# Softcap attention with a soft mixture of experts: filler products merged, and half tiles moved four products ahead

## The chip, the cores and the metric

The kernel runs on one core of one Trainium2 chip. The metric is the device time in microseconds of one execution, as the median of several runs. The profile is of one more execution.

A few names: TensorE (PE in the profile) multiplies; a product is a pair of instructions, a weight load (PEld) and the product itself. ScalarE is ACT, VectorE is DVE, GpSimd is POOL, and SyncE (SP) issues most of the loads and all stores. PSUM is the memory that products are written to, in eight banks.

## What is computed

```python
scores = scale * np.matmul(q, k.transpose(0, 1, 3, 2))     # batch 8, 12 heads, seq 448, head_dim 64
scores = cap * np.tanh(scores / cap)
attn = softmax(scores)
x = (attn @ v) reshaped to (3584, 768)

logits = x @ phi                                            # 32 slots = 8 experts x 4
slot_input = softmax(logits over tokens).T @ x
for e in range(8):
    slot_out[e] = np.maximum(slot_input[e] @ w1[e], 0) @ w2[e]    # 768 -> 1024 -> 768
return softmax(logits over slots) @ slot_out                # (3584, 768) float32
```

The output is 3584 x 768 float32, 11.0 MB.

## The kernel before

**Attention.** Heads are taken in pairs and the tokens of a pair in seven tiles. 336 such tiles in an order of their own (`order`) are cut into 56 chunks of six (`CH`), each in two halves of three. For each half, `qk_chunk` (L338) makes the scores on TensorE, `tanh_chunk` (L355) applies tanh on ScalarE straight from PSUM, and `exp_chunk` (L376) the exponential. For some chunks VectorE takes part of the exponential as a polynomial (`poly_exp`, L604). `pv_first`, `pv_tail` and `pv_rest` (L655 to L675) multiply by v and normalise. The loop over chunks (L901 to L934) writes the order out by hand: each chunk has named slots ("0", "m", "e", "a", "b", "r", "c", "d"), and `at(j, slot, ...)` (L796) hangs further work into a slot of chunk j: transposes of the next heads, weight loads, polynomial steps, the logits and slot sums of a finished batch. There is no scheduler; each engine runs its instructions in the order in which they are written.

**Filler products.** At some places TensorE is given products whose result nobody reads. `busy(n, home)` (L880) makes n of them with a 128 x 128 operand of ones. Where `home` is wider than 128 columns it makes n // 3 products of 384 columns and n % 3 of 128 instead; the wide ones read the tile `wide`, whose columns 128 to 383 GpSimd fills at L85. `spare(n, parts)` (L801) does the same into a PSUM tile of `parts` x 128 columns. At the start, L889 to L891 run 4 and then 27 narrow fillers, and `first_half(0)` (L892) then transposes the first q and k. In chunk 0, slot "c" has `spare(16, 1)`.

**Experts.** After the last chunk, the sequence at L1000 finishes the last heads. `layer1` (L1074) multiplies the slot inputs by w1 for four experts at a time, `relu` brings the result back, `h_transp` (L1090) turns it, and `layer2(n0, half)` (L1105) adds four products of w2 to one of two sums: `so_ps[0]` for the first 384 output columns, `so_ps[1]` for the other 384. Each half takes 64 products, so 16 calls of `layer2`. w2 lies partly in SBUF (`w2b`) and partly in tiles that SyncE loads back from DRAM (`w2t`, L1059).

**Output.** ScalarE copies the first sum to `so[0]` (L1168). While half 1 is being summed (L1170 to L1176), *half tiles* are already made: `half_tile(n, 0, ...)` (L1142) multiplies the slot weights of 128 tokens by `so[0]`, ScalarE or VectorE scales the result out of PSUM (L1150, L1152), and SyncE stores it (L1136), 192 KB each. They come in pairs, one on ScalarE and one on VectorE, after 16, 24, ..., 56 products of half 1, twelve half tiles in all (`NH`). Then VectorE copies the second sum to `so[1]` (L1177), the other halves of those twelve token tiles follow, and the remaining 16 token tiles are made whole (L1193 to L1205).

**What the steps of the prediction touch.** TensorE's program has 9128 instructions. Numbers of instructions are counted in that program, from its start; half 1 begins at number 8871 before the change.

Of the kernel before, what the change touches and what calls it, by code (L numbers as in the profile page):

```python
# [18 lines left out]
P = 128  # L19
# [18 lines left out]
def kernel(  # L38
# [201 lines left out]
    def first_half(h):  # L240
        for nm in ("k", "q"):
            if h == 0:
                qkT[nm, 0] = qk[0].tile([P, NT, P], BF16, name=nm + "T", tag=nm + "T")
        one = psT.tile([P, 8, P], BF16, name="ps1", tag="T")
        two = psV.tile([P, NT, P], BF16, name="ps2", tag="pv")
        if h == 0:

            three = boots[1][:, CS - 1, :].bitcast(BF16).rearrange("p (c q) -> p c q", q=P)
            first_pieces(h, (("cast", "q", 4, NT, act, None, 0), ("cast", "k", 0, CS, dve, None, 0),
                             ("cast", "q", 0, 4, dve, None, 0), ("turn", "q", 4, NT, pe, three, 0),  # L250
                             ("turn", "k", 0, CS, pe, two, 0), ("copy", "q", 4, NT, act, three, 0),
                             ("cast", "k", CS, NT, pool, None, 0),
                             ("turn", "q", 0, 4, pe, one, 0), ("copy", "k", 0, CS, dve, two, 0),
                             ("copy", "q", 0, 4, dve, one, 0), ("junk", "k", 3, 0, pe, None, 0),
                             ("turn", "k", CS, NT, pe, three, 3),
                             ("copy", "k", CS, NT, dve, three, 3)))
        else:
            first_pieces(h, (("cast", "k", 0, NT, dve, None, 0), ("cast", "q", 0, NT, dve, None, 0),
                             ("turn", "k", 0, NT, pe, two, 0), ("turn", "q", 0, NT, pe, one, 0),
                             ("copy", "k", 0, NT, dve, two, 0), ("copy", "q", 0, NT, dve, one, 0)))  # L260
            for nm in ("q", "k"):
                raws.pop((nm, 0)), casts.pop((nm, 0))
                load(nm, 2)
# [532 lines left out]
    def at(j, slot, f, *a):  # L796
        if j < 0:
            j, slot = 0, "b"
        aux.setdefault((j, slot), []).append((f, a))
# [24 lines left out]
    for b in range(B):  # L824
        j, p = b * PER, 6 * b
# [30 lines left out]
            at(j, slot, poly_exp, chunk, shared[chunk][0], n)  # L856
    for n, job in enumerate(wjobs):
        at(1 + n * (NCH - 5) // len(wjobs), "b", *job)
    for j, slot, n in ((0, "a", 5), (0, "c", 16), (1, "b", 12), (1, "c", 3)):
        at(j, slot, spare, n, 1)  # L860
    LATE = ((52, 'd', 3, 1), (54, 'd', 3, 3),)
    for j, slot, n, parts in LATE:
        at(j, slot, spare, n, parts)
# [13 lines left out]
    boots = [psS.tile([P, CS, 512], F32, name=f"boot{n}", tag="sc") for n in range(2)]  # L877
    junk = boots[0][:, 0, 0:P]

    def busy(n, home=None, by=None):  # L880
        home, by = junk if home is None else home, ones if by is None else by
        if home.shape[-1] > P:
            for _ in range(n // 3):
                pe.matmul(home, ones, wide, start=True, stop=True)
            n, home = n % 3, home[:, 0:P]
        for _ in range(n):
            pe.matmul(home, by, by, start=True, stop=True)

    busy(4, by=nc.const_aps.tensor(1.0, [P, P], BF16))  # L889
    junk = boots[1][:, 0, 0:P]  # L890
    busy(27)  # L891
    first_half(0)  # L892
    qk_chunk(0)
    qk_chunk(1)
# [56 lines left out]
    def bank(shape, dt=F32, name="bank"):  # L951
        n = turns.pop(0)
        if not turns:
            turns.extend((3, 2, 6, 0, 1))
        return big.tile(shape, dt, name=name, tag=f"b{n}")
# [149 lines left out]
    def layer2(n0, half):  # L1105
        for n in range(n0, n0 + 4):
            i, ft, gg = blocks[n]
            pe.matmul(so_ps[half][32 * gg:32 * gg + NS, :],  # L1108
                      hpad[:, 4 * i + gg, ft, :],
                      w2_half(n, half),  # L1110
                      start=(n0 == 0), stop=(n0 == len(blocks) - 4))
# [30 lines left out]
    def half_tile(n, half, home, eng):  # L1142

        bb, c = divmod(n, NT)
        if c == 0:
            obs[bb, half] = wts.tile([P, NT, HD], F32, name="obh", tag="w1", bufs=E)
        ob = obs[bb, half][:, c, :]
        pe.matmul(home, et_tile(bb, c), so[half], start=True, stop=True)  # L1148
        if eng == "dve":
            dve.tensor_scalar_mul(ob, home, winv[:, bb, c:c + 1])  # L1150
        else:
            act.mul(ob, home, winv[:, bb, c:c + 1])  # L1152
        k = waiting.pop(half, n)
        if half and n + 1 < NH and c < NT - 1 and k == n:
            waiting[half] = n
            return
        store(k, half, half + 1, obs[bb, half][:, c - (n - k):c + 1, :], n - k + 1)

    NH = 12
# [9 lines left out]
    done = 0  # L1169
    for n0 in range(0, n2, 4):  # L1170
        layer2(n0, 1)

        if n0 % 8 == 4 and n0 > 4 and done < NH:
            for eng in ("act", "dve"):
                half_tile(done, 0, bank([P, HD], name="op0"), eng)
                done += 1  # L1176
# [5 lines left out]
    for n in range(B // 2 * NT):  # L1182
        bb, c = divmod(n, NT)
# [58 lines left out]
```

## Time and profile before

| what | value |
| --- | --- |
| median of 3 runs (282.66 to 283.16) | 282.76 us |
| the profiled execution | 283.45 us |
| its span, from the first to the last instruction | 281.7 us |
| ScalarE busy | 249.1 us (88%) |
| TensorE busy, products | 246.5 us (88%) |
| VectorE busy | 239.5 us (85%) |
| moved by DMA | 68.08 MB, mean 242 GB/s |

A busy time is a share of the whole span; which engine limits a stage is read from the stage itself. In the timeline a row has start, length, engine, line, operation, what it writes and reads, the count of merged instructions, and in brackets the idle time of the engine before it with what ended it. "issue" there means that the engine waited for nothing that the profile shows. The queue q8 in the DMA part brings TensorE's own instructions.

### The profile page before, as it was taken

How to read it: one execution, taken by the hardware profiler on the slowest of the kernel's cores; microseconds unless marked ns; L12 is line 12 of the kernel's file. 1: busy time of each engine (PE TensorE's matmuls, PEld its weight loads, DVE VectorE, ACT ScalarE, POOL GpSimd, SP SyncE). 2: the span in 40 equal slices, each digit the busy share in tenths (PEclk: the TensorE clock that was granted, in tenths of full speed). 3: DMA queues.
4: the chain of work that ended last, by engine and by line, in shares of the span. 5: the costliest groups of instructions: out<-in, count | busy, mean ns of one | idle time of the engine just before them, and what ended most of it. 6: DMA issues, size and time to landing. Idle time of an engine off the chain costs nothing.

```text
span 281.7 us, 10449 instructions
## 1 busy us (share of the span) xinstructions
PE 246.5 (88%) x4563; PEld 167.0 (59%) x4563; DVE 239.5 (85%) x474; ACT 249.1 (88%) x198; POOL 140.9 (50%) x198
## 2 busy tenths in 40 slices
PE   8897889998998999889998999899988999997720
PEld 7555556756665766566656675667565777642410
DVE  3479999999999999999999999999999996447840
ACT  3999999999999999999999999999999997236730
POOL 7885548662957285727673768285744120200000
PEclk9999999999999999999999999999999999999995
DMA  7999999999999999999999999999999589959997
GB/s 245 245 190 203 218 211 227 228 223 217 206 218 225 219 231 226 225 216 213 221 226 215 207 220 230 217 219 214 231 217 220 128 260 317 408 201 391 413 424 303
DMA packets 58332, 68.08 MB, mean 242 GB/s; under 512 B 4144, under 2 KB 54448, under 8 KB 58288
## 3 DMA queue, kind: packets, MB, share of 16 engines
q0 software_dynamic: 42448, 35.31, 79.7%
q1 hardware_dynamic: 15552, 31.89, 32.4%
q8 instruction: 35, 0.57, 0.7%
q10 hardware_dynamic: 288, 0.23, 0.3%
q14 instruction: 9, 0.07, 0.1%
HBM read 91.72 MB, written 19.27 MB: 394 GB/s over the span
## 4 chain that ended last, share of the span: by engine, by line
ACT 38%; PE 31%; DVE 20%; issue 5%; POOL 1%; DVEq 0%; ACTq 0%
ACT ex L374 16%; ACT ex L366 14%; PE pv L635 8%; ACT ex L362 7%; PE sc L349 4%; DVE xq L645 2%; DVE xp L615 2%; PE so_ps L1108 2%; PE hp L1080 2%; DVE xp L613 2%; DVE ex L616 2%; ACT ob L1202 2%; PE op L1193 1%; DVE xf L612 1%; PE op L1148 1%
## 5 line engine op out<-in xcount | busy, mean ns | idle before, releaser
L366 ACT ACTIVATE ex<-sc 128x1344 f16<-128x1344 f32 (+1 forms) x91 | 118.5, 1405 | 1.5 <-PE sc L349 1.5
L374 ACT ACTIVATE ex<-ex 128x1344 bf16<-128x1344 f16 (+5 forms) x58 | 110.2, 1911 | 0.1
L635 PE MATMUL pv<-vbd,ex 128*128 128x130 bf16 (+1 forms) x1610 | 95.0, 212 | 9.5 <-POOL vbd L289 3.9
L635 PEld LDWEIGHTS <-ex 128*128 128x128 bf16 (+1 forms) x1680 | 75.6, 101 | 38.1 <-issue 6.2
L289 POOL CAST vbd<-vraw 64x896 bf16<-64x896 f32 x46 | 47.3, 1027 | 60.2 <-PE pv L635 42.5
L349 PE MATMUL sc<-qT,kT 64*64 64x448 bf16 x672 | 66.4, 359 | 5.6 <-ACT ex L366 4.1
L349 PEld LDWEIGHTS <-kT 64*64 64x64 bf16 x672 | 22.4, 105 | 14.4 <-ACT ex L366 6.3
L645 DVE TENSOR_TENSOR xq<-pv,rec 128x448 bf16<-128x448 f32 x46 | 28.7, 625 | 1.6
L362 ACT ACTIVATE ex<-sc 128x2688 f16<-128x2688 f32 x11 | 28.1, 2552 | 0.1
L615 DVE TENSOR_TENSOR xp<-xp,xf 128x1344 f16<-128x1344 f16 (+2 forms) x34 | 27.5, 808 | 0.5
L616 DVE TENSOR_TENSOR ex<-ex,xp 128x1344 uint16<-128x1344 uint16 (+2 forms) x34 | 26.9, 791 | 0.2
L613 DVE TENSOR_TENSOR xp<-xf 128x1344 f16<-128x1344 uint16 (+2 forms) x34 | 26.9, 790 | 0.2
L116 POOL DMA_DIRECT2D w1b<-in_moe_w_dram x32 | 25.8, 808 | 0.0
L281 DVE COPY kT<-kps 128x896 bf16<-128x896 bf16 x23 | 14.2, 616 | 4.9 <-PE kps L276 2.8
L610 DVE TENSOR_SCALAR ex<-ex 128x1344 uint16<-128x1344 f16 (+2 forms) x34 | 17.0, 501 | 1.2 <-ACT ex L362 0.7
L614 DVE TENSOR_SCALAR xp<-xp 128x1344 f16<-128x1344 f16 (+2 forms) x34 | 17.0, 500 | 0.6
L612 DVE TENSOR_SCALAR xf<-ex 128x1344 uint16<-128x1344 uint16 (+2 forms) x34 | 17.2, 507 | 0.3
L185 POOL DMA_DIRECT2D qb<-in_q_dram x22 | 16.3, 739 | 1.5 <-PE qps L279 0.9
L297 POOL MEMSET vbd<- 64x1 bf16 x22 | 3.0, 138 | 27.7 <-PE pv L635 27.4
L617 DVE TENSOR_SCALAR ex<-ex 128x1344 uint16<-128x1344 uint16 (+2 forms) x34 | 16.5, 484 | 0.2
L185 POOL DMA_DIRECT2D kb<-in_k_dram x22 | 16.5, 748 | 0.0
L120 POOL DMA_DIRECT2D w2d<-in_moe_w_dram x21 | 16.1, 789 | 0.0
(124 smaller groups left out, 320.6 us busy)
## 6 DMA issues: line engine op xcount, KB each, us to landing
w1b<-in_moe_w_dram POOLq DMA_DIRECT2D x32, 384.0 KB, 9.6
vraw<-in_v_dram SPq DMA_DIRECT2D x44, 224.0 KB, 6.3
w2d<-in_moe_w_dram POOLq DMA_DIRECT2D x21, 384.0 KB, 9.7
w2t<-w2d SPq DMA_DIRECT2D x21, 384.0 KB, 6.5
out_dram<-ob SPq DMA_DIRECT2D x7, 768.0 KB, 6.8
qb<-in_q_dram POOLq DMA_DIRECT2D x22, 224.0 KB, 8.1
kb<-in_k_dram POOLq DMA_DIRECT2D x22, 224.0 KB, 7.7
w2b<-in_moe_w_dram POOLq DMA_DIRECT2D x11, 384.0 KB, 8.9
```

The source lines that it names most:

```text
L116: pool.dma_start(out=w1b[e][:, js, fs], in_=w1r[:, e, js, fs])
L185: pool.dma_start(out=t, in_=quad_ap(nm, Q))
L289: pool.tensor_copy(vbds[Q % 2][r, :, :, c0:c0 + DH], raw[r])
L349: ins = pe.matmul(sc[cs, u, 0:S], qkT["k", Q][r, c, cs], qkT["q", Q][r, :, cs], start=True, stop=True).ins
L362: apart["t", i - 1] = apart["t", i] = act.activation(exs[j].bitcast(F16), own["board"][:, :, 0:S], ACT.Tanh, scale=qk_scale / cap).ins
L366: ins = act.activation(exs[j][:, half * CS + u0:half * CS + u1, :].bitcast(F16), (own[0] if i == u0 == 0 else sc)[:, u0:u1, 0:S], ACT.Tanh ...
L374: act.activation(exs[j][:, u0:u1, :], exs[j][:, u0:u1, :].bitcast(F16), ACT.Exp, scale=cap)
L613: lambda: dve.tensor_tensor(p, s, s.bitcast(F16), op=ALU.mult),
L615: lambda: dve.tensor_tensor(p, p, s, op=ALU.mult),
L616: lambda: dve.tensor_tensor(y, y, p, op=ALU.add),
L635: pe.matmul(out_, exs[j][r, u, q0:q0 + (HP if tail else P)], v_, start=(c == 0 and g == gs[0] < NF), stop=(c == NT - 1), skip_group_check= ...
L645: dve.tensor_tensor(xq[Q][:, h, s0:s1, :], pv[:, 0:s1 - s0, 0:DH], rec.to_broadcast([P, s1 - s0, DH]), op=ALU.mult)
```

## The change

Three places.

```diff
-    for j, slot, n in ((0, "a", 5), (0, "c", 16), (1, "b", 12), (1, "c", 3)):
-        at(j, slot, spare, n, 1)
+    for j, slot, n, parts in ((0, "a", 5, 1), (0, "c", 16, 3), (1, "b", 12, 1), (1, "c", 3, 1)):
+        at(j, slot, spare, n, parts)
...
     busy(4, by=nc.const_aps.tensor(1.0, [P, P], BF16))
     junk = boots[1][:, 0, 0:P]
-    busy(27)
+    busy(5)
+    busy(22, boots[1][:, 0, 0:3 * P])
...
     for n0 in range(0, n2, 4):
         layer2(n0, 1)
 
-        if n0 % 8 == 4 and n0 > 4 and done < NH:
+        if n0 % 8 == 0 and n0 > 0 and done < NH:
             for eng in ("act", "dve"):
                 half_tile(done, 0, bank([P, HD], name="op0"), eng)
```

At the start, 22 of the 27 narrow fillers become 7 of 384 columns and 1 of 128. In slot "c" of chunk 0, 16 narrow ones become 5 of 384 columns and 1 of 128. Both together are 24 weight loads and 24 products less, 48 instructions, and the columns that pass through TensorE are as many as before. The pairs of half tiles now come after 12, 20, ..., 52 products of half 1. On the other four engines the order of instructions and their waits are what they were.

## The prediction, made before the result was known

> **What bounds the kernel now.** I read four views, in this order: the page (how long the span is and what the DMA engines move in each slice), the stage table by windows (which resource is full in which stage), the timeline of the stage in which the half tiles begin, and the DMA view in windows of about a microsecond, to find single packets.
>
> The page first: the span, and the row for the queue that brings TensorE its instructions.
>
> ```profile
> span 281.7 us, 10449 instructions
> ...
> PE 246.5 (88%) x4563; PEld 167.0 (59%) x4563; DVE 239.5 (85%) x474; ACT 249.1 (88%) x198; POOL 140.9 (50%) x198
> ...
> q8 instruction: 35, 0.57, 0.7%
> ```
>
> The profiled execution took 283.45 us, so 1.75 us lie around its span; it stands 0.69 us above the median of 282.76. All sums below are differences, and I take them off the median.
>
> Now the stage table (columns: stage, length, busy time of PE, PEld, DVE, ACT, POOL with instruction counts, granted TensorE clock, DMA share, GB/s).
>
> ```profile
> 6.44:236.50 230.06, 211.45 (x4105) 147.33 (x4101) 215.47 (x423) 229.51 (x167) 134.35 (x180) 1.00 1.19 220
> ...
> 249.20:252.50 3.30, 2.83 (x44) 0.82 (x36) 0.87 (x3) 1.47 (x3) 0.00 (x0) 1.00 0.13 46
> 252.50:253.50 1.00, 1.00 (x15) 0.28 (x12) 0.75 (x2) 0.71 (x2) 0.00 (x0) 1.00 0.62 229
> 253.50:256.30 2.80, 2.64 (x34) 0.66 (x30) 2.04 (x5) 1.78 (x4) 0.00 (x0) 1.00 1.05 395
> 256.30:258.30 2.00, 1.04 (x5) 0.50 (x6) 1.57 (x4) 0.60 (x2) 0.00 (x0) 1.00 1.05 393
> ...
> 270.00:275.00 5.00, 0.56 (x4) 0.10 (x2) 1.94 (x2) 0.90 (x1) 0.00 (x0) 1.00 1.02 424
> 275.00:280.00 5.00, 0.00 (x0) 0.00 (x0) 0.00 (x0) 0.00 (x0) 0.00 (x0) 0.50 0.95 395
> 280.00:281.70 1.70, 0.00 (x0) 0.00 (x0) 0.00 (x0) 0.00 (x0) 0.00 (x0) 0.50 0.00 2
> ```
>
> There are two regimes. From 6.44 to 236.5 ScalarE is busy for 229.51 of 230.06 us: the attention phase is as long as ScalarE's work, and what TensorE saves there is worth nothing unless it moves ScalarE's start. From 253.5 to 280 the DMA engines are full with output stores, and the last 5 us hold nothing else. The end is therefore the moment at which the store stream starts plus its bytes over its rate. Between the two, from 249.2 to 252.5, the DMA engines are almost empty (share 0.13): the weight loads are over and no output exists. A microsecond taken out of the way to the first store is a microsecond off the end, as long as the stream then never runs dry.
>
> So the timeline around the first stores carries the argument.
>
> ```profile
> 248.48 1.14 PE L1108 MATMUL so_ps<-w2t,hpad 128*32 128x384 bf16 x21
> 250.09 0.83 PE L1108 MATMUL so_ps<-w2t,hpad 128*32 128x384 bf16 x15 [0.47 <-issue]
> 250.85 0.50 PE L1148 MATMUL op<-so,ET 128*128 128x384 bf16 x2
> 251.28 0.51 PE L1108 MATMUL so_ps<-w2t,hpad 128*32 128x384 bf16 x8
> 251.72 0.50 PE L1148 MATMUL op<-so,ET 128*128 128x384 bf16 x2
> ...
> 249.52 0.48 ACT L1168 CAST so<-so_ps 128x384 bf16<-128x384 f32 x1 [2.53 <-PE so_ps L1108]
> 251.22 0.58 ACT L1152 ACTIVATE obh<-op,winv 128x384 f32<-128x384 f32 x1 [1.23 <-PE op L1148]
> ...
> 251.83 0.34 SPq L1136 DMA_DIRECT2D out_dram<-obh  x1
> ```
>
> Row one holds the last 20 products of half 0 and the first of half 1. Then TensorE stands for 0.47 us "issue": it waits for nothing that the profile shows. In the program's order the instruction after the gap is number 8873 of TensorE's 9128, a weight load on which no wait stands. I read the gap as TensorE's instruction stream not having arrived. Page row q8: 35 packets and 0.57 MB for 9126 instructions, so about 260 instructions a packet; I take the power of two beside it, 256, as the size of a block (an estimate). And the packet before the gap is there, in this one-microsecond window of the DMA view:
>
> ```profile
> ## 3 DMA queue, kind: packets, MB, share of 16 engines
> q1 hardware_dynamic: 143, 0.39, 99.0%
> q8 instruction: 1, 0.02, 5.5%
> ```
>
> That is 247.6 to 248.6, with the engines 99% full of weight loads; the next window with such a packet is 251.0 to 252.6. The packet comes some 1.5 us ahead of the end of the gap.
>
> **The change part by part.**
>
> *Fewer instructions.* 22 start-up products become 7 wide and 1 narrow (14 pairs of load and product less), 16 in chunk 0 become 5 and 1 (10 pairs less): 24 pairs, 48 instructions. At the start:
>
> ```profile
> 1.16 3.08 PE L887 MATMUL boot<-ones 128*128 128x128 bf16 x27
> 4.20 0.53 PE L236 MATMUL boot<-ident,casts 128*64 128x128 bf16 x3
> ...
> 1.45 0.31 POOL L85 MEMSET ones<- 128x256 bf16 x1
> ...
> 3.79 0.35 ACT L232 CAST casts<-qraw 128x192 bf16<-128x192 f32 x1 [0.85 <-DMA qraw<-in_q_dram]
> ...
> 6.44 2.54 ACT L366 ACTIVATE ex<-sc 128x448 f16<-128x448 f32 x3 [1.20 <-PE sc L349]
> ```
>
> The 27 issue about every 0.107 us. Five narrow ones end at 1.16 + 5 x 0.107 = 1.70. The first wide one reads columns that GpSimd writes until 1.76, a new wait, with all of TensorE queued behind it: about 1.81. I take the wide product at three times the narrow pace (the other end, one narrow pace each, would only end earlier): 1.81 + 22 x 0.107 = 4.16. The transposes of q start at 4.20, after ScalarE's cast (3.79 + 0.35). So the cost is between 0 and 0.05 us; I take 0. The cover is the arrival of q; if it were gone, each microsecond here would move ScalarE's first tanh at 6.44 and with it everything.
>
> In chunk 0:
>
> ```profile
> 10.22 1.07 PE L887 MATMUL junk<-ones 128*128 128x128 bf16 x16
> 11.22 0.76 PE L349 MATMUL sc<-qT,kT 64*64 64x448 bf16 x6
> ...
> 15.87 0.82 PE L884 MATMUL junk<-ones 128*128 128x384 bf16 x4
> 16.54 0.28 PE L887 MATMUL junk<-ones 128*128 128x128 bf16 x2
> ```
>
> Sixteen narrow take 11.22 - 10.22 = 1.00 us; a wide one takes (16.54 - 15.87) / 4 = 0.17, so 5 wide and 1 narrow take 0.90. TensorE gains 0.10 us in front of scores that end at 11.98, while ScalarE is busy without a break from 6.44: worth 0.
>
> *The block boundary.* The boundary stays at instruction 8873, but 48 instructions less stand ahead of it, so another instruction is number 8873. Half 1 now begins at 8823: 12 products (24 rows), a pair of half tiles (4), 8 products (16), a second pair (4), one more product (2), then the boundary. The gap, if there is one, falls behind two pairs instead of ahead of all of them. Is there one? The block takes time to come:
>
> ```profile
> 244.68 0.36 PE L1097 MATMUL hps<-ident,hb 128*128 128x16 bf16 x8
> 244.96 1.27 PE L1080 MATMUL hp<-w1b,slT 128*32 128x256 bf16 x40
> ```
>
> 256 instructions ahead of the gap, at 244.7, lies the boundary before it; from there to the resumption at 250.09 are 5.4 us. 48 instructions later TensorE is in the second row, at about 245.35 (7 pairs of the first row and 17 of the second). The same 5.4 us give 250.75. It is needed when two pairs and one product are done. Pairs follow each other by 251.72 - 250.85 = 0.87 us, so that is about 1.3 us after the first pair.
>
> *The half tiles.* Without the gap the 11 other products run on from 249.62 at the latest, at (250.85 - 250.09) / 15 = 0.051 us: 250.18; the first half tile also needs the cast of so, which ends at 250.00, plus about 0.05. So the first pair starts between 250.05 and 250.18 instead of 250.85: 0.67 to 0.80 us earlier, and I take 0.75. The second pair and one product are then done at about 251.4, 0.6 us after the block is there: no gap left. Without the stall's removal the four products fewer alone would be worth 4 x 0.051 = 0.2 us. What is late next: the cast on ScalarE, then the evictions, which keep their pace of a pair in 0.87 us.
>
> *The stream.* A pair is two stores:
>
> ```profile
> out_dram<-obh SPq DMA_DIRECT2D x14, 192.0 KB, 2.0
> ...
> 255.63 0.51 PE L1108 MATMUL so_ps<-w2t,hpad 128*32 128x384 bf16 x8
> ...
> 256.27 0.55 DVE L1177 CAST so<-so_ps 128x384 bf16<-128x384 f32 x1
> ```
>
> 393 KB in 0.87 us are made, at 393 GB/s they drain in 1.0 us, so the stream fills once it has begun. After the last pair there are now 12 products and no longer 8 ahead of VectorE's cast of the second half: the pair 0.75 earlier, 4 products more, cast at 256.27 - 0.75 + 0.05 or so. The share stays at 1.05 through that hole today, and the hole grows by 0.05. Hidden.
>
> Fetch boundaries move in the attention phase too, which is the one cost that no row shows directly. Its bounds: ScalarE's idle there is 0.55 us in all, so at most 0.5 is won. For the loss, the stretch where 256 instructions will stand in the shortest time:
>
> ```profile
> 163.57:168.74 5.17, 5.17 (x134) 3.92 (x129) 4.94 (x11) 5.17 (x5) 2.72 (x5) 1.00 1.26 222
> ...
> 168.99 0.56 PE L349 MATMUL sc<-qT,kT 64*64 64x448 bf16 x6
> ...
> 169.41 2.54 ACT L366 ACTIVATE ex<-sc 128x1344 f16<-128x1344 f32 x2
> ```
>
> If a block needs 5.4 us, TensorE stands 0.2 us at 168.7; the scores at 168.99 serve the second tanh of the last row, at 169.41 + 1.2, so 1.0 us covers it. I take 0, with 0.5 either way.
>
> Sum: 0 + 0 - 0.75 + 0 = -0.75 us. From the profiled execution 283.45 that is 282.70; from the median 282.76 it is 282.01, so **282.0**.
>
> [...]
>
> **The rivals.**
>
> *The gap belongs to half 1 and stays.* For it: the profile names no releaser, and the gap sits exactly behind half 1's first product. Against it: no wait stands on the instruction, and the packet and the count fit. Then only the four products are won: -0.2, 282.55.
>
> *The block comes late again.* The gap falls behind the second pair. For it: the engines are full until 249. Four stores (4 x 192 KB, 2.0 us at 393 GB/s) are out by then, so a gap of 0.5 leaves a hole of about 0.3 in the stream: -0.45, 282.3.
>
> *Slower: the start.* The narrow products at 1.16 go at 0.107 us each, those at 10.22 at 0.063: TensorE begins at a slower pace, though the granted clock in the rows says 1.00 throughout. If the wait for GpSimd breaks the run and TensorE stays slow beyond 5.4 us, where it speeds up now, the work between there and the tanh at 6.44 (about 1.0 us) doubles, and the next scores with it: +1.0 to +2.5, I take 1.5, so +0.75 net and 283.5. It decides from 0.75 us on. Against it: the break is 0.1 us long. [...]
>
> *More than forecast.* ScalarE's waits in the attention phase shrink as well: up to 0.5 more, 281.5.
>
> **How the numbers follow.** Forecast 0.60 (own range 281.6 to 282.4), gap stays 0.13, block late 0.10, slower 0.12, more 0.05. A measurement of this kernel tells about 0.2% (0.57 us) from no change: faster means below 282.2, slower above 283.3. The forecast lies near that edge: of its 0.60 I count 0.53 as faster and 0.07 as same. Faster 0.53 + 0.05 + 0.02 of the late block = 0.60; same 0.07 + 0.13 + 0.08 = 0.28; slower 0.12. The range leaves out most of the slower case and the far end of the better one: 281.5 to 283.0.
>
> **What would show it.** In the changed profile: the twelve first products of half 1 in one run without "issue" between them; the cast of so as what the first half tile waits for; the first eviction near 250.5 and the first store near 251.1; a DMA share over 0.9 from about 252.8 to 279.3; ScalarE's first tanh still at 6.44 and its idle in the attention phase still about half a microsecond. Wrong if a gap stands ahead of the first pair, if the first tanh is late, or if the store stream has a hole; or if the stream starts 0.75 earlier and the end does not.

## The result and the profile after

The changed kernel takes 283.43 us (median of 13 runs, 283.07 to 285.14); the kernel before took 282.66 us in 13 runs beside it (281.67 to 283.36). The ratio, that of the means, is 1.004 (95% interval 1.0022 to 1.0057): slower by about 0.4%, where 0.3% faster was forecast. The medians differ by less, 0.77 us (0.3%): nine runs of the change lie at 283.1 to 283.5, four at 284.3 to 285.1. What is special in those four is not known. The median span went from 280.7 us (35 runs of before, beside the first experiments) to 281.7 (13 runs of after).

Yet nearly all that was forecast up to the first store is in the profile after (283.27 us, span 281.5, so close to its median). First TensorE's timeline there (start, length, engine, line, operation, count): the last 20 products of half 0 and the first 12 of half 1 are one unbroken row, and the first pair follows.

```profile
248.29 1.47 PE L1109 MATMUL so_ps<-w2t,hpad 128*32 128x384 bf16 x32
249.86 0.48 PE L1149 MATMUL op<-so,ET 128*128 128x384 bf16 x2
250.27 0.51 PE L1109 MATMUL so_ps<-w2t,hpad 128*32 128x384 bf16 x8
```

The "issue" row is gone. ScalarE's rows in the same stage:

```profile
249.33 0.48 ACT L1169 CAST so<-so_ps 128x384 bf16<-128x384 f32 x1 [2.54 <-PE so_ps L1109]
250.22 0.58 ACT L1153 ACTIVATE obh<-op,winv 128x384 f32<-128x384 f32 x1 [0.41 <-PE op L1149]
```

From the start of the cast of so to the first eviction are 250.22 - 249.33 = 0.89 us, before 251.22 - 249.52 = 1.70: 0.81 us won against this profile, just over the 0.67 to 0.80 of the prediction. Now SyncE's issues of stores, each from a window of its own:

```profile
250.82 0.34 SPq L1137 DMA_DIRECT2D out_dram<-obh  x1
...
251.73 1.55 SPq L1137 DMA_DIRECT2D out_dram<-obh  x1
...
253.38 0.38 SPq L1137 DMA_DIRECT2D out_dram<-obh  x1
```

The third store takes 1.55 us to issue where its neighbours take 0.34 to 0.42. The stage table (stage, length, busy PE, PEld, DVE, ACT, POOL, clock, DMA share, GB/s) shows what follows:

```profile
249.20:251.40 2.20, 2.11 (x36) 0.67 (x28) 0.76 (x2) 1.37 (x3) 0.00 (x0) 1.00 0.10 39
251.40:252.70 1.30, 1.30 (x20) 0.35 (x12) 1.05 (x2) 0.85 (x2) 0.00 (x0) 1.00 0.82 293
252.70:253.90 1.20, 1.20 (x16) 0.36 (x18) 0.69 (x3) 0.78 (x2) 0.00 (x0) 1.00 0.13 41
253.90:256.30 2.40, 1.73 (x24) 0.55 (x17) 1.75 (x3) 0.96 (x2) 0.00 (x0) 1.00 1.05 393
...
279.00:280.00 1.00, 0.00 (x0) 0.00 (x0) 0.00 (x0) 0.00 (x0) 0.00 (x0) 0.50 0.68 273
```

The stream starts, stops at 252.7 for 1.2 us (share 0.13) while three more half tiles lie ready (they are scaled by 252.74), and is full again at 253.9. Before, it was full from 253.5 or so. It ends at 280.00, where it ended at 280.15. And the DMA view of 251.4 to 252.95 names who is there:

```profile
q1 hardware_dynamic: 271, 0.37, 64.5%
q8 instruction: 1, 0.02, 5.9%
```

One packet of TensorE's instructions, from 251.45 to 252.91 in the trace. That it is a fetch which follows the crossing of the boundary is the author's reading, from times alone: in the five profiles in which TensorE stands at the boundary, such a packet begins 1.03 to 1.15 us after TensorE goes on, and in the change 0.3 us after the boundary's place by count. What it brings, the trace does not say. Against the profile before, the packet came 0.33 us later and the first store 1.01 us earlier, so that now they meet.

The packets in the hole tell more. As the instruction packet ends, at 252.90, a row of eight store packets of 1.5 KB begins. Each one starts when the one before it ends (to 0.02 us), the eighth ends at 253.79, and only then do the others go on.

```profile
252.90:253.78 0.88, 0.88 (x15) 0.24 (x18) 0.62 (x1) 0.59 (x2) 0.00 (x0) 1.00 0.05 12
```

A share of 0.05 to 0.06 is about what one engine of 16 gives (1/16 = 0.0625), and the eight packets, 12 KB, are a sixteenth of a store of 192 KB. The instruction packet's own 5.9% of 16 engines over 1.55 us come to 1.46 us of one engine, the packet's length. The author's reading, that one DMA engine carried both and was late with its part of a store, rests on these numbers alone. The same row of eight stands behind the packet in merge_only, no_start_merge and late_less (runs below). No record names the engine of a packet, and why the other store packets come only after these eight is not shown.

The attention phase was not harmed. ScalarE there is idle 229.53 - 229.33 = 0.20 us; in the profile before it was 0.55, in two more profiles of that kernel 0.17 and 0.20:

```profile
6.67:236.20 229.53, 211.89 (x4095) 147.18 (x4091) 216.18 (x423) 229.33 (x167) 133.96 (x180) 1.00 1.19 219
```

### The profile page after: what moved, and what is told of

It is laid out like the page before. It is cut to its first block, busy times and chain, and to the rows that moved or that the text cites. A ratio compares the mean times of both kernels' runs of the same rounds, so it can differ in the third digit from the quotient of the medians.

```text
span 281.5 us, 10401 instructions
## 1 busy us (share of the span) xinstructions
PE 247.0 (88%) x4539; PEld 166.0 (59%) x4539; DVE 240.3 (85%) x474; ACT 248.9 (88%) x198; POOL 140.7 (50%) x198
## 4 chain that ended last, share of the span: by engine, by line
ACT 45%; PE 26%; DVE 19%; issue 5%; DMA 1%; POOL 0%; DVEq 0%; ACTq 0%
ACT ex L374 18%; ACT ex L366 16%; ACT ex L362 8%; PE pv L635 6%; PE sc L349 4%; DVE xq L645 3%; DVE xp L615 2%; PE hp L1081 2%; DVE xp L613 2%; PE so_ps L1109 2%; DVE xf L612 2%; DVE ex L610 2%; PE op L1149 1%; DVE qT L281 1%; DMA out_dram<-obh 1%
## 5 line engine op out<-in xcount | busy, mean ns | idle before, releaser
L362 ACT ACTIVATE ex<-sc 128x2688 f16<-128x2688 f32 x11 | 28.1, 2550 | 0.1
L614 DVE TENSOR_SCALAR xp<-xp 128x1344 f16<-128x1344 f16 (+2 forms) x34 | 18.3, 538 | 0.6
```

What stands on the lines that cost most here:

```text
L362: apart["t", i - 1] = apart["t", i] = act.activation(exs[j].bitcast(F16), own["board"][:, :, 0:S], ACT.Tanh, scale=qk_scale / cap).ins
```

## The experiments

Three theories. HOLE: the instruction packet that follows the boundary now meets the first stores, and the stream loses about what it had won, or more. START: the wide fillers make the beginning slower; the first tanh stands at 6.67 in the profile after and stood at 6.44. COUNT: shifted boundaries cost something in the attention phase. Each ratio below is to the kernel before, run on the same chip beside it. Half 1 begins 2 instructions ahead of the boundary in the kernel before, by the place of the gap; "the boundary at +50" means 50 instructions behind the beginning of half 1, which is its place in the change by count. Blocks are counted as 256 instructions, the prediction's estimate; from the start of the first q8 packet to that of the last, TensorE has 8667 products and weight loads in the profile of before and 8679 in that of the change, 254.9 and 255.3 for each of the 34 packets.

### Only the start fillers merged (start_only)

```diff
-    busy(27)
+    busy(5)
+    busy(22, boots[1][:, 0, 0:3 * P])
```

> Only the start fillers are merged (28 instructions less). Theory START (the wide fillers leave TensorE longer at its slow pace, ScalarE's first tanh moves from 6.44 to about 6.7, in some runs later): slower by 0.3 to 1.0 us, first tanh after 6.6. Theory HOLE (the loss sits in the store stream: the instruction packet meets the first stores and SyncE's issue stands): the pairs stay behind the boundary, so within 0.3 us of before, first tanh wherever it is.

Measured: 282.89 us, ratio 1.0012 (0.9997 to 1.0028). The first tanh is at 6.96 here, but also at 6.86 in a profile of the kernel before and at 6.43 in a kernel with the same merged start: its place changes from run to run. The boundary falls at +30, and there TensorE stands. Here are the last four of half 1's first sixteen products: three begin by 250.07, the sixteenth at 250.49, 0.42 us behind them.

```profile
250.07 0.76 PE L1109 MATMUL so_ps<-w2t,hpad 128*32 128x384 bf16 x4
```

So the gap moved by the 28 instructions that went. The packet, 251.64 to 252.59, ends as the first store's data begin, and the second store takes 0.79 us to issue. The medians differ by 0.08 us, as HOLE had it, but the interval reaches to 0.8 us, so that this run alone does not exclude START's loss.

### Only the half tiles moved (half_only)

```diff
-        if n0 % 8 == 4 and n0 > 4 and done < NH:
+        if n0 % 8 == 0 and n0 > 0 and done < NH:
```

> Only the half tiles are moved, no instruction less: the gap of about 0.5 us stays behind the first product of half 1. First pair about 0.2 us earlier than before. Theory START: -0.2 us, first tanh at 6.44. Theory HOLE: the packet lies where it was, the stores 0.2 us nearer to it; between -0.2 and +0.2 us.

Measured: 282.74 us, ratio 0.9998 (0.9982 to 1.0013). Its profile shows the gap at less than half the size, and the packet (DMA view, 250.7 to 251.8) ahead of any store data:

```profile
249.70 0.67 PE L1108 MATMUL so_ps<-w2t,hpad 128*32 128x384 bf16 x11 [0.22 <-issue]
```

```profile
q8 instruction: 1, 0.02, 5.3%
issues: line engine op xcount, KB each, median us to landing
out_dram<-obh SPq DMA_DIRECT2D x2, 192.0 KB, 1.9
```

Two stores were issued in that window and no queue but q8 moved a packet in it. None of the first eight stores took over 0.42 us to issue. The four products alone are worth nothing that these runs can tell. START's -0.2 us lies in the interval too, so the run does not separate the theories.

### Both merges, half tiles where they were (merge_only)

> 48 instructions less, half tiles where they were: the boundary falls behind the first pair and 7 products. Theory START: slower by 0.3 to 1.0 us at the first tanh, less about 0.5 for the gap that is gone. Theory HOLE: the packet meets the stores of the first pairs, SyncE's issue stands over 1 us, the end is where it was.

The edit is the change without its last hunk. Measured: 283.58 us, ratio 1.0028 (1.0015 to 1.0041). First tanh at 6.43, as early as before, and still slower, by 0.77 us in the medians: against START, which put the loss there. HOLE had the stalled issue right and the time wrong, for it expected the end where it was. The third store:

```profile
251.48 1.68 SPq L1137 DMA_DIRECT2D out_dram<-obh  x1
```

### The change with the narrow start and the same count (no_start_merge)

```diff
     busy(27)
...
+    for j, slot, n, parts in ((0, "a", 5, 3), (0, "c", 16, 3), (1, "b", 12, 3), (1, "c", 3, 3)):
...
+    LATE = ((52, 'd', 3, 3), (54, 'd', 3, 3),)
```

> The changed kernel with the 27 narrow start fillers back, and 48 instructions saved at other fillers (chunks 0, 1 and 52), so that the boundary falls behind two pairs as in the change. Theory START: first tanh at 6.44 again, and faster than before by 0.3 to 0.8 us. Theory HOLE: SyncE's third store issue stands about 1.5 us as in the change, and the gain over before is under 0.3 us; not slower than before by more than 0.3.

Measured: 283.56 us, ratio 1.0029 (1.0015 to 1.0043). START had this one faster than before by 0.3 us or more. It is as slow as merge_only, with the start of the kernel before: START falls. HOLE missed the time again: it allowed 0.3 us over before, and the medians differ by 0.75. One store stands as long as in the change, here the fourth:

```profile
252.07 1.57 SPq L1136 DMA_DIRECT2D out_dram<-obh  x1
```

### The kernel before, twice more (before_again, before_third)

> The kernel before, a second profile. Theory HOLE (a packet of TensorE's instructions that meets the first stores makes SyncE's issue stand until about 0.37 us after the packet's end): the median run of before is 282.8 and the first profile was 283.45 with a stall of 0.62 us; a run near the median has the packet ended before the second store is issued, no issue over 0.5 us, and its first megabyte stored about 4.1 us after the first eviction instead of 4.3.

> The kernel before, a third profile, for the spread of the packet's time: theory HOLE expects the span to follow the end of the packet, theory CHANCE (the runs differ by when loads land and the clock rises at the start) the first tanh.

The profile that the prediction used was 0.69 us above its median, and it matters what was special in it. The second profile took 283.70 us, the third 283.07, and both are above the 282.48 of the runs beside them. The gap behind the first product, in the second and then in the third:

```profile
250.21 0.83 PE L1108 MATMUL so_ps<-w2t,hpad 128*32 128x384 bf16 x15 [1.00 <-issue]
```

```profile
249.76 0.83 PE L1108 MATMUL so_ps<-w2t,hpad 128*32 128x384 bf16 x15 [0.17 <-issue]
```

In the third the last packet ran from 250.85 to 251.98, the first store was issued at 251.50, no issue stood, and the stream ended at 279.65. In the second it ran from 251.31 to 252.64, a store stood for 0.63 us and the stream ended at 280.27. So the span went with the packet, as HOLE had it. But it went with the gap too, which sets when the stores begin: of the 0.50 us between the ends of the first and the third, 0.33 are there at the first store. These runs do not part the two. The first tanh points the other way (6.44 in the slower, 6.86 in the faster one): in these three, CHANCE, which put the difference down to the start, does not hold.

### 84 instructions more (narrow_half, narrow_only)

```diff
-    def spare(n, parts=3):
+    def spare(n, parts=1):
```

narrow_half has the half tiles moved as well.

> All wide spare fillers made narrow (84 instructions more ahead), half tiles moved as in the change. The boundaries now fall inside half 0 and behind the half tiles. Theory HOLE: the packet is there before the first stores, no store issue over 0.5 us, first eviction about 0.9 us after the cast of so begins, first megabyte about 4.1 us after the first eviction; faster than before by 0.3 to 0.8 us. Theory COUNT (any shift of the boundaries costs through the attention phase): slower than before, store stream or not.

> The same 84 instructions more, half tiles where they were: first eviction about 1.1 us after the cast of so begins (four products more than in narrow_half). Theory HOLE: faster than before by 0.1 to 0.6 us, about 0.2 us behind narrow_half. Theory COUNT: slower than before.

Measured: 284.24 us, ratio 1.0082 (1.0056 to 1.0107), and 284.56 us, ratio 1.0073 (1.0054 to 1.0092). HOLE as stated here failed: both are slower, as COUNT had it. The profile shows why. The first stores are free, as expected. But by the same count a second boundary comes 256 instructions after the first, at +174, and the packet from 257.80 to 259.21 meets the middle of the stream. narrow_half, SyncE's issue and the stages:

```profile
258.45 1.16 SPq L1136 DMA_DIRECT2D out_dram<-obh  x1
```

```profile
254.00:257.00 3.00, 2.33 (x27) 0.77 (x26) 2.06 (x5) 1.18 (x3) 0.00 (x0) 1.00 1.05 392
...
258.00:259.00 1.00, 0.84 (x3) 0.29 (x3) 0.78 (x2) 0.96 (x2) 0.00 (x0) 1.00 0.66 249
259.00:260.00 1.00, 0.82 (x4) 0.29 (x3) 0.99 (x2) 0.71 (x2) 0.00 (x0) 1.00 0.56 198
260.00:261.00 1.00, 0.86 (x6) 0.39 (x5) 0.62 (x1) 0.98 (x2) 0.00 (x0) 1.00 0.89 330
```

The store's issue ends at 259.61; in narrow_only the packet is at 258.63 to 260.00 and a store stands for 1.35 us. So it is not the first stores alone that are tender: behind this packet, in the middle of the stream, stands a hole as well (share 0.66 and 0.56 in the rows above). This pair lost more than the change did, and some of it ahead of the stores: from the first tanh to the last exponential it takes 230.28 and 230.75 us, where the profiles of the other runs have 229.5 to 230.1 (late_less apart), and the cast of so begins 13.2 us after the last exponential, where it is 13.0 to 13.1 in the others. That part is COUNT's, or that of the added products themselves; the runs do not say.

### The change with its boundary put back (late_restore, late_restore_2)

```diff
-                at(j + k, slot, f, n)
+                at(j + k, slot, f, n, *((1,) if f is spare and b > 0 else ()))
```

Everything of the change, and six calls of `spare(7)` made narrow between its start and the tail, so that the 48 instructions are back before half 1 begins.

> The changed kernel (both merges, half tiles moved), but the wide fillers of six later chunks made narrow: 48 instructions come back in the attention phase, 8 in each of six batches, so that the boundary in the tail is where it was before the change. Theory HOLE: the packet comes ahead of the first stores, no store issue over 0.6 us, and the time is that of half_only: within 0.3 us of before. Theory COUNT or START (the loss sits in the attention phase or the start): still slower than before by 0.5 us or more.

> late_restore once more, as the candidate for a version that beats both. If its first ratio (0.9985) was no chance: between 0.997 and 1.000 again, no store issue over 0.6 us. If it was chance: around 1.000 or above.

Measured: 282.57 us, ratio 0.9985 (0.9969 to 1.0001), and 282.70 us, ratio 0.9996 (0.9982 to 1.0011). The loss is gone. START and COUNT kept it, for the merged start and the shifted boundaries of the first batches are all still there. This is the nearest pair to the change: what the tail computes is the same, and the boundary is at +2 in place of +50. In the first profile no gap is left and the packet lies in the empty time ahead of the stores:

```profile
248.26 1.66 PE L1109 MATMUL so_ps<-w2t,hpad 128*32 128x384 bf16 x32
...
249.85 0.50 PE L1149 MATMUL op<-so,ET 128*128 128x384 bf16 x2
```

```profile
250.83 0.34 SPq L1137 DMA_DIRECT2D out_dram<-obh  x1
```

```profile
251.00:252.00 1.00, 1.00 (x12) 0.23 (x10) 0.70 (x2) 0.61 (x2) 0.00 (x0) 1.00 0.32 121
252.00:253.00 1.00, 1.00 (x15) 0.34 (x18) 0.62 (x1) 0.71 (x2) 0.00 (x0) 1.00 0.98 367
253.00:254.00 1.00, 1.00 (x18) 0.25 (x14) 0.75 (x2) 0.71 (x2) 0.00 (x0) 1.00 1.05 392
...
279.00:280.00 1.00, 0.00 (x0) 0.00 (x0) 0.00 (x0) 0.00 (x0) 0.00 (x0) 0.50 0.00 0
```

The first store is issued at 250.83, as in the change (250.82), and the stream ends a microsecond earlier, at 279.04. As a kernel it beats the change; over the kernel before, no gain is shown (medians 0.06 and 0.22 us lower, both intervals reach 1).

### 48 instructions less, late (late_less)

```diff
-                at(j + k, slot, f, n)
+                at(j + k, slot, f, 1 if b == 6 and n == 25 else n)
```

Left out are 24 fillers whose result nobody reads.

> The kernel before with 24 of the 25 narrow fillers of chunk 49 left out (their result is read by nobody): 48 instructions less, all in the last chunks, start and half tiles untouched. Theory HOLE: the boundary falls where merge_only has it, the packet meets the first stores, one store issue of over 1 us, slower than before by 0.5 to 1.0 us. Theory COUNT or START: like before, within 0.3 us.

Measured: 284.02 us, ratio 1.0058 (1.0035 to 1.0082), and a store that stands for 1.61 us in a profile of 285.85 us. The stall is HOLE's prediction, but the loss of 1.39 us is more than its 0.5 to 1.0, and the run does not prove it: from 210 to 215 us the granted clock is 0.66 here, where it is 1.00 in the first profile of before, and that may cost as well.

```profile
205.00:210.00 5.00, 3.10 (x64) 2.38 (x62) 4.94 (x10) 5.00 (x4) 1.67 (x3) 1.00 1.28 222
210.00:215.00 5.00, 4.77 (x56) 3.35 (x55) 3.55 (x10) 4.13 (x4) 0.37 (x2) 0.66 1.27 224
```

A mean clock of 0.66 for 5 us, and ScalarE, never idle in the row above, is idle for 0.87 us.

### The first pair right behind the gap (half_first)

```diff
-        if n0 % 8 == 4 and n0 > 4 and done < NH:
+        if n0 % 8 == 0 and done < NH:
```

> The kernel before with the pairs of half tiles after 4, 12, ..., 44 products of half 1, so that the first pair comes right behind the gap, about 0.6 us earlier than before. If earlier stores were worth their whole lead: -0.6 us. Theory HOLE: the packet still comes at about 251 and now meets the second or third store, SyncE's issue stands until 0.4 us after the packet's end, and the gain is between -0.3 and +0.5 us.

Measured: 282.84 us, ratio 1.0012 (0.9994 to 1.0031). The lead is not paid out. In its profile, though, the packet came early (250.20 to 251.13), no gap and no stalled issue is left, and the stream runs dry elsewhere: behind the last early pair 20 products now stand ahead of VectorE's cast of the second sum, and no data move for half a microsecond.

```profile
258.20:258.70 0.50, 0.36 (x2) 0.10 (x1) 0.45 (x2) 0.50 (x2) 0.00 (x0) 1.00 0.00 0
```

That is part of the lead; the cast of the first sum was also 0.23 us later here than in the first profile of before.

### A second queue for some stores (two_queues, pool_queue)

```diff
-        store(k, half, half + 1, obs[bb, half][:, c - (n - k):c + 1, :], n - k + 1)
+        store(k, half, half + 1, obs[bb, half][:, c - (n - k):c + 1, :], n - k + 1,
+              act if half == 0 and eng == "act" and n < 6 else sp)
```

> The changed kernel, with the first three stores of ScalarE's half tiles issued from ScalarE's queue and VectorE's from SyncE's. Theory QUEUE (only SyncE's queue stands while the packet runs, the DMA engines are free): ScalarE's stores go out meanwhile, the hole in the stream (share 0.25 for a microsecond) is filled by half or more, faster than the changed kernel by 0.4 us or more, so within 0.4 us of before. Theory ENGINE (one DMA engine is held by the packet, and every store needs all engines): both queues stand, the first megabyte is stored over 5 us after the first eviction as in the change, slower than before by 0.5 us or more.

Measured: 290.70 us, ratio 1.0274 (1.0254 to 1.0293), by another cause: one of SyncE's loads of w2 stood in a wait of 13.0 us that ends with a store of half tiles, and five loads were issued only behind the first stores. Why that wait arose was not tested.

```profile
253.02 2.26 SPq L1060 DMA_DIRECT2D w2t<-w2d  x5
```

It says nothing on the question. pool_queue has `pool` in the place of `act` and leaves SyncE's waits for w2 as they are.

> The changed kernel with the first three stores of ScalarE's half tiles issued by GpSimd, which is idle there; SyncE's queue keeps the other stores and the same waits for w2. Theory QUEUE (SyncE's queue alone stands while the packet runs): GpSimd's stores go out meanwhile and SyncE's stall is shorter or gone; the first megabyte is stored within 4.6 us of the first eviction, and the time is within 0.4 us of before. Theory ENGINE (the engine that carries the packet holds every store up): the share of the DMA engines drops to about a quarter for a microsecond as in the change, first megabyte after more than 5 us, slower than before by 0.5 us or more.

Measured: 283.39 us, ratio 1.0025 (1.0004 to 1.0046). SyncE's store stands half as long, and the hole is nearly filled:

```profile
252.45 0.79 SPq L1137 DMA_DIRECT2D out_dram<-obh  x1
```

```profile
252.00:253.00 1.00, 1.00 (x18) 0.23 (x10) 0.75 (x2) 0.71 (x2) 0.69 (x2) 1.00 0.89 338
253.00:254.00 1.00, 1.00 (x15) 0.35 (x12) 0.75 (x2) 0.68 (x2) 0.06 (x1) 1.00 0.92 344
```

QUEUE is right about the hole and wrong about the time. GpSimd's stores do go out meanwhile, and the kernel is as slow as with the hole; the last store packets end at 279.89, in the change at 280.00. The end of the stream shows where the microsecond went:

```profile
279.00:279.50 0.50, 0.00 (x0) 0.00 (x0) 0.00 (x0) 0.00 (x0) 0.00 (x0) 0.50 0.06 25
279.50:280.00 0.50, 0.00 (x0) 0.00 (x0) 0.00 (x0) 0.00 (x0) 0.00 (x0) 0.50 0.05 18
```

From 279.06 to 279.88 seven packets of 3 KB go one after another, each when the one before it ends, at a share of 0.05 to 0.06, again about that of one engine of 16; in the change the share is 1.05 from 279.00 to 279.50. That fits the author's reading of one DMA engine late with its part of the stores, here until the end; no record names the engine.

## Why the prediction was wrong

**Put side by side.** From the first store's issue to the last store packet in the trace, for every profile but two_queues, whose stores waited for loads:

| profile | first store | its first data | last packet of the stream | length | last instruction packet |
| --- | --- | --- | --- | --- | --- |
| before, third | 251.50 | 252.35 | 279.65 | 28.1 | 250.85 to 251.98 |
| half_only | 251.28 | 252.12 | 279.50 | 28.2 | 250.81 to 251.74 |
| late_restore | 250.83 | 251.68 | 279.04 | 28.2 | 250.40 to 251.35 |
| late_restore_2 | 250.95 | 251.79 | 279.16 | 28.2 | 250.11 to 251.03 |
| before, as predicted from | 251.83 | 252.67 | 280.15 | 28.3 | 251.12 to 252.51 |
| before, second | 251.95 | 252.79 | 280.27 | 28.3 | 251.31 to 252.64 |
| start_only | 251.74 | 252.58 | 280.20 | 28.5 | 251.64 to 252.59 |
| half_first | 251.25 | 252.09 | 279.78 | 28.5 | 250.20 to 251.13 |
| pool_queue | 250.78 | 251.63 | 279.89 | 29.1 | 251.51 to 252.88 |
| the change | 250.82 | 251.66 | 280.00 | 29.2 | 251.45 to 252.91 |
| merge_only | 250.56 | 251.40 | 279.85 | 29.3 | 251.38 to 252.78 |
| narrow_half | 251.31 | 252.15 | 280.85 | 29.5 | 257.80 to 259.21 |
| narrow_only | 252.00 | 252.84 | 281.63 | 29.6 | 258.63 to 260.00 |
| no_start_merge | 250.67 | 251.51 | 280.36 | 29.7 | 251.64 to 253.27 |
| late_less | 252.68 | 253.53 | 282.65 | 30.0 | 254.25 to 256.06 |

Where the packet has ended when the first store's data begin to move (in start_only it ends just then), the stream takes 28.1 to 28.5 us; where it runs while data move, 29.1 to 30.0.

**The fewer instructions.** Right: the start costs nothing that could be told (no_start_merge is as slow without the merged start, late_restore has it and no loss), and the wide fillers began at 1.80 us, where 1.81 was worked out.

**The block boundary.** Right in its place: the gap of start_only stands at +30, and in the change none is left. In the five profiles with a gap TensorE goes on 1.3 to 1.6 us after the end of the instruction packet before it, whatever the gap's size, which fits the reading that it waits for instructions; the profile names no releaser for the gap ("issue"). But read from one profile, the gap's size was not the kernel's, and this is a second step that failed: the -0.75 of the sum rests on a gap of 0.47 us, and the next two profiles of before have 1.00 and 0.17. In half_only and half_first, whose programs are the same up to there, it is 0.22 and none. In the third profile of before the way from the cast to the first eviction is 250.90 - 249.49 = 1.41 us and not 1.70, so that 0.5 us is there to be won and not 0.8; an ordinary run, faster than all three, may have less. Nor are the four products worth 0.2 where no gap is: merge_only, with its pairs after 16 products, takes 0.91 us from the cast to the first eviction and the change 0.89.

**The half tiles.** Right: the first pair at 249.86, 0.53 us after the cast began, against 0.53 to 0.66 forecast. It starts 0.05 us behind the end of the cast, which is what it waited for, as forecast.

**The stream.** This step failed first of all. The prediction had it that "the stream fills once it has begun", called what was left "Hidden" and put it at 0; it looked for a hole only where production pauses. It followed the instruction packet as something that TensorE waits for, never as something that takes a share of the DMA engines (5.9% of 16 over 1.55 us in the change). In the change the packet runs while the first stores move, and the stream takes 29.2 us in place of 28.2: 1.0 us lost. The nearest pair says the same in whole runs: against the kernel before, the medians of the change are 0.77 us higher, those of late_restore 0.06 and 0.22 lower, so 0.8 to 1.0 us go with the boundary's place. The way to the first store won little against that, for late_restore has it as well and shows no gain. The prediction's own signs of being wrong named the outcome, a hole in the stream and an end that does not come earlier; no term of its sum held it.

**The attention phase.** Within the 0.5 us either way. ScalarE's idle is 0.20 us in the change against 0.55 in the profile before, but 0.17 and 0.20 in the other two profiles of before, so nothing of it is shown to be the change's.

**The rivals.** "The block comes late again" saw a gap behind the second pair, in TensorE; there was none. "Slower: the start" gave 283.5, and 283.43 was measured: that is luck, for it named the wrong place. That a short break keeps TensorE slow, and that its work then doubles, was the author's estimate, and no run shows it: the two paces read, 0.107 and 0.063 us, differ by a factor of 1.7, and the granted clock is recorded as full from 5.98 us in the change, between the 5.39 and 6.52 of the profiles of before. No rival held what happened. At the boundary TensorE stood 0.17 to 1.00 us in the profiles of before and not at all in late_restore (28.2 us of stream); where the packet meets the stores, the stream took 29.1 us and more.

## What to carry to other kernels

Here 28 instructions less moved TensorE's gap by 28 places (start_only), and with 48 less the packet fell among the first stores: after a change in the count of instructions, ask where each packet of instructions falls, and not only whether the engine waits for it. In this kernel the stage full of stores (share 1.05) had no free place for such a packet, with streams of 29.1 to 30.0 us, and the stage ahead of it (share 0.13 before) had one, with 28.1 to 28.5. And before a gap in one profile is put into a sum as its whole size, look whether the profiled run is a usual one: this one was 0.69 us above its median, and the gap may have been part of the reason.

## What the runs showed of the hardware

In these six profiles a stalled store's issue ends 0.36 to 0.40 us after the end of an instruction packet. From the trace: the change 252.91 and 253.28, merge_only 252.78 and 253.16, no_start_merge 253.27 and 253.64, narrow_half 259.21 and 259.61, pool_queue 252.88 and 253.24, the first profile of before 252.51 and 252.88. Not every store that is issued while a packet runs stands: in the first profile of before the one at 251.83 took 0.34 us, in late_less the one at 254.40 took 0.33, and the next one stood. What decides it is open.

An instruction packet mostly took 0.88 to 1.0 us (the median is 0.95 in the profile before), single ones among loads up to 1.94 (no_start_merge, from 233.84); those that ran while store data moved took 1.37 (pool_queue) to 1.82 (late_less).

The time from which the granted clock is recorded as full at the start differs from run to run of one kernel: 5.39, 5.47 and 6.52 us in the three profiles of before, and 4.62 and 6.17 in the two of late_restore. Ahead of that no clock is recorded, so the 1.00 of earlier rows, which the prediction leant on, says nothing.
